# A selective-attention and SwiGLU kernel on one Trainium2 core: a reordered first batch, bias rows issued by GpSimd, delayed stores

## The chip, the cores and the metric

The kernel runs on one core of one Trainium2 chip. The core has five engines with a queue each, which run in parallel and meet at semaphores: TensorE (PE; its weight loads are listed apart as PEld), VectorE (DVE), ScalarE (ACT), GpSimd (POOL) and SyncE (SP), which here only issues DMAs. 16 DMA engines move data between device memory and the on-chip memory SBUF. Matrix products land in PSUM, eight banks per partition, and are read from there by DVE and ACT. The metric is device microseconds of one execution. Each engine works through its own queue in program order; an instruction that waits holds up all behind it on that engine.

## What is computed

Eight batches of eight heads of causal attention over 576 positions with head size 64; a bias made of a cumulative sum of the positive part of `s` is added to the scores. The result, as 4608 tokens of width 512, goes through a SwiGLU block with 1536 hidden features.

```python
scores = scale * np.matmul(q, k.transpose(0, 1, 3, 2))
cum = np.cumsum(np.maximum(s, 0.0), axis=-1)
bias = -(cum[:, :, :, None] - cum[:, :, None, :])
scores = np.where(causal, -1000000000.0, scores + np.minimum(bias, 0.0))
attn = np.exp(scores - np.max(scores, axis=-1, keepdims=True))
attn = attn / (np.sum(attn, axis=-1, keepdims=True) + 1e-09)
x = heads side by side of np.matmul(attn, v)
g = x @ w_gate
out = (g * (1.0 / (1.0 + np.exp(-g))) * (x @ w_val)) @ w_out
```

## The kernel before

**Layout.** The 64 heads are handled in 16 blocks of four (`hb`, or `h` in the later loops). The two tile pairs `KQ[hb % 2][r]` hold the transposed k and q of a block: for r = 0 and 1 two heads, in 64 of 128 partitions. Four of the other 64 partitions hold bias rows: high and low part of the cumulative sum and constants, so that the score matmul (L347) adds the bias by itself. The rest of them has to be zero; memsets at the start see to it (L203 and L209 on GpSimd, L204 on ACT, which multiplies the tile of ones `one_s` by 0). `aug` (L180 to L188) sends the four bias rows of a block from `HL` to `KQ` with four DMAs. `HL` comes from `s` through a chain on VectorE (L213 to L217), whose cumulative sum takes `one_s` too.

**Preparing a block.** `load_qk` loads k and q in float32, `cast_one` or `cast_half` turn them to bfloat16 (tiles `ck`, `cq`). For blocks 0 to 4 TensorE transposes them (`pe_transpose`, L272; `pe_transpose_half`, L286) and `pe_out` copies from PSUM to `KQ`, on DVE (L301) or ACT (L299). `prep_one` is one such transpose with its DVE and its ACT copy. For blocks 5 to 15, `scratch` writes the cast tiles to device memory (L244), `transposes` reads them back with transposing DMAs (L254), and `split` copies them to `KQ` on DVE (L259). `load_v` loads V of a batch in five pieces (L164), into one buffer; `cast_v` casts them to `VT` (L171). `init_vt` sets the ones column and the zero border of `VT`.

**A head.** `score_piece` makes the scores of a head in four pieces, the exps on ACT (L360) and the causal masks on GpSimd (L363 for four diagonal blocks, L368 for the last small one). In the first batch two pieces share a two-bank PSUM tile and one exp. `av_piece` multiplies by V (L385), `av_out` divides by the row sums (L401, L402), and `x_pe` transposes a pair of heads (L420) and copies the result to the FFN's input `xt` (L424, L425).

**Order.** The program writes the order out by hand: the order of the calls is the order in each queue. `first_batch` (L588 to L620) runs heads 0 to 7 alone. In it a dictionary `avq` says after which head's scores which products come, and `wq` when GpSimd loads the FFN weights (L315, float32 to bfloat16). After that, for each of nine FFN tiles of 512 tokens, `ffn_items` yields 36 times, and between its pieces `pump` runs pieces of `attn_items` for the next batch: in proportion to the count n of yields, from n0 on (7 in the first tile). `hook` hangs preparation on certain n of the first tile. `side` places loads, casts, bias rows, scratch writes and DMA transposes by the head's number in its block (`step`). An FFN tile has 12 feature blocks of gate (L518, tanh on ACT at L523, first product on DVE at L525) and value (L533, second product `ht` on DVE at L538), then four output blocks (L546), each scaled on ACT (L554) and stored by SyncE (L556).

Of the kernel before, what the change touches and what calls it, by code (L numbers as in the profile page):

```python
# [19 lines left out]
def kernel(  # L20
# [11 lines left out]
    nc = tc.nc  # L32
# [60 lines left out]
    VT = [const.tile([128, NCH, H, D + 1], BF16, name=f"vt{i}") for i in range(2)]  # L93
    ident = const.tile([128, 128], BF16)
    s_sb = const.tile([BH, S], FP32)
    one_s = const.tile([BH, S], FP32)
    c8 = const.tile([BH, S], FP32)
    HL = const.tile([BH, 4, 2, S], BF16)
    warm = const.tile([128, 1], FP32)
# [1 line left out]
    with tc.manual_schedule():  # L101
# [52 lines left out]
        def load_qk(hb):  # L154
            load_one(hb, "k")
            load_one(hb, "q")
# [31 lines left out]
                )  # L188

        nc.sync.dma_start(s_sb, s.rearrange("b h n -> (b h) n"))  # L190
        for r in range(NR):
            load_one(0, "k", (r, r + 1))
            load_one(0, "q", (r, r + 1))
        load_qk(1)

        nc.vector.memset(warm, 0.0)
        nc.scalar.activation(warm, warm, AF.Exp)
        nc.vector.memset(one_s, 1.0)
        nc.vector.memset(HL[:, 0:2, 0, :].bitcast(FP32), ONES2)
        nc.vector.memset(HL[:, 2:4, 1, :].bitcast(FP32), NEGS2)  # L200
        make_identity(nc, ident)
        for r in range(2):
            nc.gpsimd.memset(aug_rows(0, r), 0.0)  # L203
            nc.scalar.mul(  # L204
                KQ[1][r][64 * (1 - r) : 64 * (1 - r) + 64, 0, :],
                one_s[:, 0:1].to_broadcast([64, NR * S + 64]), 0.0,
            )
        for r in range(2):
            nc.gpsimd.memset(aug_rows(1, r)[:, 1, :], 0.0)  # L209
            for i in range(2):  # L210
                nc.gpsimd.memset(KQ[i][r][64 * r : 64 * r + 64, :, NR * S :], 0.0)

        nc.vector.tensor_scalar(s_sb, s_sb, 0.0, 8.0, ALU.max, ALU.mult)  # L213
        nc.vector.tensor_tensor_scan(c8, one_s, s_sb, 0.0, ALU.mult, ALU.add)
        nc.vector.tensor_copy(HL[:, 0, 1, :], c8)
        nc.vector.tensor_sub(HL[:, 1, 1, :], c8, HL[:, 0, 1, :])
        nc.vector.tensor_copy(HL[:, 2:4, 0, :], HL[:, 0:2, 1, :])  # L217

        SP4 = [nc.sync] * 4

        cts = {}

# [170 lines left out]
        def av_out(bh):  # L393
# [13 lines left out]
            give(bs)  # L407
            pts.pop(bh)

        def x_pe(pr):  # L410
            b, r = divmod(pr, H // 2)
            ot = ots.pop(pr)
            for tt in ((0, 1) if b == 0 else (b + 1,)):
                if r == 0:
                    xts[tt] = xtp.tile([128, 4, TT], BF16, tag="xt", name="xt")
# [12 lines left out]
        def side(h, step):  # L428
            bh = HB * h + step
            if bh == 8:  # L430
                w_load("o", 0)
            if bh == 10:
                w_load("o", 1)
            if bh == H:
                for c in range(5):
                    cast_v(1, c, nc.gpsimd)
            if h >= 3 and h + 3 < NHB and step == 0:
                load_qk(h + 3)
            if h + 1 < NHB and h + 1 >= NPE:
                if step == 0:  # L440
                    split(h + 1, "k", nc.vector)
                    aug(h + 1, SP4)
                if step == 1:
                    split(h + 1, "q", nc.vector)
            if h + 2 < NHB and h + 2 >= NPE:
                if step == 1:
                    cast_one(h + 2, "k", nc.gpsimd)
                if step == 2:
                    cast_one(h + 2, "q", nc.gpsimd)
                    scratch(h + 2)  # L450
                if step == 3:
                    transposes(h + 2)
            bn = h // 2 + 1
            if 2 <= bn < B:
                if h % 2 == 0:
                    if step == 2:
                        load_v(bn, (0, 1))
                    if step == 3:
                        load_v(bn, (2, 3, 4))
                else:  # L460
                    if step == 1:
                        cast_v(bn, 0, nc.gpsimd)
                        cast_v(bn, 1, nc.gpsimd)
# [10 lines left out]
            pe_out(hb, nm, g, 0, nc.vector)  # L474
            pe_out(hb, nm, g, 1, nc.scalar)

        PREP_AT = {(0, 3): 0, (1, 3): 1, (2, 1): 2, (2, 3): 3}

        def attn_items():
            for kk in range(H, BH + 2):  # L480
                h, step = divmod(kk, HB)
                if kk < BH:
# [1 line left out]
                        cast_one(h + 2, "k", nc.gpsimd)  # L484
                        cast_one(h + 2, "q", nc.gpsimd)
                    if step == 0 and 3 < h + 1 < NPE:
                        aug(h + 1, SP4)
                    for ci in range(4):
                        score_piece(kk, ci)
                        if ci == 1:  # L490
                            side(h, step)
                        yield kk + 0.1 + ci / 8
                        if h + 1 < NPE and (step, ci) in PREP_AT:
                            prep_one(h + 1, PREP_AT[step, ci])
                            yield kk + 0.1 + ci / 8
                x = kk - 2
                if x >= H and x % 2 == 1:
                    x_pe(x // 2)
                    yield kk + 0.5
                p = kk - 1  # L500
                if H <= p < BH:
# [5 lines left out]
                    av_out(p)  # L507
                    yield kk + 0.8

        def ffn_items(tt):  # L510
            xt = xts[tt]
            hts = []
            for ft in range(NFT):
                j, f0 = divmod(ft * 128, WCH)
                gbs = take()
# [26 lines left out]
            for ts_ in range(4):  # L542
                ybs = take()
                py = view(ybs, DM)
                for ft in range(NFT):
# [7 lines left out]
                ysb = yp.tile([128, DM], FP32, tag="y", name="ysb")  # L553
                nc.scalar.mul(ysb, py, 0.5)  # L554
                give(ybs)
                nc.sync.dma_start(  # L556
                    out[tt * TT + ts_ * 128 : tt * TT + (ts_ + 1) * 128, :], ysb
                )
                yield 1

        def init_vt(i):
            nc.gpsimd.memset(VT[i][:, :, :, D : D + 1], 1.0)
            nc.gpsimd.memset(VT[i][64:128, 4, :, 0:D], 0.0)

        cast_half(0, "k", 0, nc.scalar)
        cast_half(0, "q", 0, nc.gpsimd)
        aug(0, SP4)
        load_v(0, range(5))
        load_qk(2)
        aug(1, [nc.gpsimd] * 4)  # L570
        for nm in ("k", "q"):
            for g in range(2):
                pe_transpose_half(0, nm, g, 0)
        pe_out(0, "k", 0, 0, nc.scalar)
        pe_out(0, "k", 1, 0, nc.scalar)
        pe_out(0, "q", 0, 0, nc.vector)
        pe_out(0, "q", 1, 0, nc.scalar)
        cast_half(0, "k", 1, nc.scalar)
        cast_half(0, "q", 1, nc.vector)
        for nm, eng in (("k", nc.scalar), ("q", nc.vector)):  # L580
            for g in range(2):
                pe_transpose_half(0, nm, g, 1)
                pe_out(0, nm, g, 1, eng)
        cast_one(1, "k", nc.gpsimd)
        cast_one(1, "q", nc.vector)
        init_vt(0)

# [39 lines left out]
        def pump(upto):  # L627
# [3 lines left out]
                except StopIteration:  # L631
                    state["pos"] = 1e9

        LAG = 1.65
        hook = {
            1: [lambda: cast_one(2, "k", nc.gpsimd), lambda: cast_one(2, "q", nc.vector)],
            2: [lambda: prep_one(2, 0)],
            3: [lambda: prep_one(2, 1)],
            4: [lambda: prep_one(2, 2)],
            5: [lambda: prep_one(2, 3)],  # L640
            8: [lambda: cast_one(3, "k", nc.gpsimd), lambda: cast_one(3, "q", nc.gpsimd)],
            21: [lambda: load_qk(5)],
        }
        for tt in range(NTT):
            lo = H * (tt + 1) + (LAG if tt else 0)
            hi = min(H * (tt + 2) + LAG, BH + 2)
# [39 lines left out]
```

The softmax here doesn't subtract the row's maximum and nothing guards it: scores larger than these inputs give would overflow.

## Time and profile before

| | us |
|---|---|
| median of 13 runs (lowest, highest) | 409.43 (406.83, 410.7) |
| the profiled execution, whole | 410.7 |
| its span in the profile | 409.0 |
| first score matmul | 11.26 |
| last piece of V 0 landed | 25.30 |
| first FFN matmul | 37.73 |
| last matmul ends | 405.29 |
| PE busy from 100 to 300 | 198.3 of 200 |

The span is the stretch from the first to the last instruction that the profile shows. Busy time is shown by engine; a busy TensorE at a granted clock of 0.50 does half the work. "Landed" is when an instruction that waits for a DMA can go on. In groups of instructions a line reads: line, engine, operation, what is written and read, count, busy time, mean, and the idle time before with what ended it.

### The profile page before, as it was taken

How to read it: one execution, taken by the hardware profiler on the slowest of the kernel's cores; microseconds unless marked ns; L12 is line 12 of the kernel's file. 1: busy time of each engine (PE TensorE's matmuls, PEld its weight loads, DVE VectorE, ACT ScalarE, POOL GpSimd, SP SyncE). 2: the span in 40 equal slices, each digit the busy share in tenths (PEclk: the TensorE clock that was granted, in tenths of full speed). 3: DMA queues.
4: the chain of work that ended last, by engine and by line, in shares of the span. 5: the costliest groups of instructions: out<-in, count | busy, mean ns of one | idle time of the engine just before them, and what ended most of it. 6: DMA issues, size and time to landing. Idle time of an engine off the chain costs nothing.

```text
span 409.0 us, 7999 instructions
## 1 busy us (share of the span) xinstructions
PE 381.2 (93%) x3047; PEld 213.2 (52%) x3100; DVE 249.1 (61%) x487; ACT 212.1 (52%) x407; POOL 125.5 (31%) x225
## 2 busy tenths in 40 slices
PE   3747798999999999999999999999999999999996
PEld 2545355665555555555555555555555554444442
DVE  7726666746873688358844884579447743752860
ACT  7823567766554555456545564565555542322321
POOL 6943263643252226131623162316211110000000
PEclk9959989999999999999999999999999999999999
DMA  7999899487745693469346926690520002002002
GB/s 245 161 257 213 272 158 217 185 253 194 193 116 182 165 229 101 129 220 231 101 122 210 262 78 109 217 183 30 116 80 0 2 27 78 0 7 98 2 1 103
DMA packets 85288, 56.71 MB, mean 139 GB/s; under 512 B 65489, under 2 KB 69553, under 8 KB 85249
## 3 DMA queue, kind: packets, MB, share of 16 engines
q1 hardware_dynamic: 81440, 51.44, 45.9%
q0 software_dynamic: 3808, 4.76, 7.0%
q8 instruction: 24, 0.39, 0.4%
q14 instruction: 16, 0.12, 0.1%
HBM read 37.90 MB, written 15.93 MB: 132 GB/s over the span
## 4 chain that ended last, share of the span: by engine, by line
PE 85%; DVE 5%; DMA 3%; ACT 2%; issue 2%; SPq 1%; POOL 0%; ACTq 0%; DVEq 0%
PE bank L546 23%; PE bank L518 21%; PE bank L533 21%; PE bank L347 9%; PE bank L385 7%; DMA rawv<-in_v_dram 3%; PE bank L420 3%; ACT th L523 1%; DVE kq L301 1%; DVE pp L525 1%; PE one L385 1%; DVE ht L538 1%; DMA s_sb<-in_s_dram 1%; ACT kq L299 1%; PE wide L347 1%
## 5 line engine op out<-in xcount | busy, mean ns | idle before, releaser
L360 ACT ACTIVATE pt<-bank 128x512 bf16<-128x512 f32 x224 | 104.2, 505 | 42.4 <-PE bank L347 35.1
L525 DVE SCALAR_TENSOR_TENSOR pp<-th,bank 128x512 bf16<-128x512 bf16 x108 | 74.2, 687 | 64.3 <-ACT th L523 63.8
L518 PE MATMUL bank<-xt,wg 128*128 128x512 bf16 x417 | 110.4, 380 | 1.5 <-DVE xt L425 0.7
L533 PE MATMUL bank<-xt,wv 128*128 128x512 bf16 x410 | 109.9, 381 | 1.1
L523 ACT ACTIVATE th<-bank 128x512 bf16<-128x512 f32 x108 | 64.6, 598 | 80.7 <-PE bank L518 78.9
L546 PE MATMUL bank<-wo,ht 128*128 128x512 bf16 x416 | 103.5, 379 | 0.9
L363 POOL TENSOR_SCALAR_AFFINE_SELECT pt<-pt 128x512 bf16<-128x512 bf16 x64 | 40.8, 638 | 126.4 <-ACT pt L360 126.3
L538 DVE TENSOR_TENSOR ht<-pp,bank 128x512 bf16<-128x512 bf16 x108 | 73.8, 684 | 7.4
L347 PE MATMUL bank<-kq 128*128 128x128 bf16 (+4 forms) x504 | 66.7, 241 | 3.6 <-DVE kq L301 2.9
L347 PEld LDWEIGHTS <-kq 128*128 128x128 bf16 x576 | 46.1, 100 | 43.9 <-issue 8.0
L518 PEld LDWEIGHTS <-wg 128*128 128x128 bf16 x432 | 38.5, 98 | 36.5 <-issue 1.3
L533 PEld LDWEIGHTS <-wv 128*128 128x128 bf16 x432 | 38.8, 98 | 34.5 <-issue 0.6
L546 PEld LDWEIGHTS <-ht 128*128 128x128 bf16 x432 | 38.2, 98 | 34.9
L385 PEld LDWEIGHTS <-pt 128*128 128x128 bf16 x960 | 41.6, 99 | 19.0 <-issue 1.9
L385 PE MATMUL bank<-vt,pt 128*128 128x65 bf16 x840 | 44.0, 194 | 0.0
L554 ACT ACTIVATE ysb<-bank 128x512 f32<-128x512 f32 x36 | 21.5, 598 | 42.9 <-PE bank L546 41.4
L368 POOL TENSOR_SCALAR_AFFINE_SELECT pt<-pt 128x64 bf16<-128x64 bf16 x64 | 15.3, 239 | 63.4 <-ACT pt L360 60.7
L402 DVE TENSOR_TENSOR ot<-bank,rc 128x320 bf16<-128x320 f32 x56 | 27.5, 491 | 1.9
L424 DVE COPY xt<-bank 128x128 bf16<-128x128 bf16 (+6 forms) x28 | 9.0, 321 | 31.7 <-PE bank L420 31.0
L171 POOL CAST vt<-rawv 128x512 bf16<-128x512 f32 (+1 forms) x40 | 25.9, 673 | 3.6 <-DMA rawv<-in_v_dram 3.6
L401 DVE RECIPROCAL rc<-bank 128x5 f32<-128x5 f32 x56 | 10.6, 190 | 25.2 <-PE bank L385 25.2
L230 POOL CAST ck<-rawk 128x1152 bf16<-128x1152 f32 x15 | 17.4, 1159 | 10.6 <-DMA rawk<-in_k_dram 10.6
(59 smaller groups left out, 192.5 us busy)
## 6 DMA issues: line engine op xcount, KB each, us to landing
out_dram<-ysb SPq DMA_DIRECT2D x36, 256.0 KB
rawk<-in_k_dram SPq DMA_DIRECT2D x15, 576.0 KB
rawq<-in_q_dram SPq DMA_DIRECT2D x15, 576.0 KB
rawv<-in_v_dram SPq DMA_DIRECT2D x32, 256.0 KB
ks<-ck SPq DMA_DIRECT2D x11, 288.0 KB
qs<-cq SPq DMA_DIRECT2D x11, 288.0 KB
wg<-in_moe_w_gate_dram POOLq DMA_DIRECT2D x2, 768.0 KB, 12.4
wv<-in_moe_w_val_dram POOLq DMA_DIRECT2D x2, 768.0 KB, 12.7
```

The lines of the kernel that those rows point to most:

```text
L171: eng.tensor_copy(VT[b % 2][0:n, c, :, 0:D], loaded["v", b][0:n, c, :, :])
L347: nc.tensor.matmul(sc[:, o : o + w], T[:, 1, e * S + 128 * tj : e * S + 128 * (tj + 1)], T[:, 0, e * S + lo : e * S + hi], start=True, sto ...
L360: nc.scalar.activation(pt[:, c0 : c0 + W], sc[:, 0:W], AF.Exp, scale=0.125)
L363: nc.gpsimd.affine_select(pt[:, 1088:1600], pt[:, 1088:1600], pattern=[[0, 4], [1, 128]], compare_op=ALU.is_ge, fill=zreg, base=0, channel ...
L385: nc.tensor.matmul(av[:, bi * (D + 1) : (bi + 1) * (D + 1)], pt[:, c0 : c0 + 128], VT[b % 2][:, tj, h, :], start=(tj == 0), stop=(tj == bi),)
L402: nc.vector.tensor_mul(ot[:, :, e * D : (e + 1) * D], av3[:, :, 0:D], rc[:, :, None].to_broadcast([128, NCH, D]),)
L518: nc.tensor.matmul(pg, WG[j][:, c, f0 : f0 + 128], xt[:, c, :], start=(c == 0), stop=(c == 3),)
L523: nc.scalar.activation(th, pg, AF.Tanh, scale=0.5)
L525: nc.vector.scalar_tensor_tensor(pp, in0=th, scalar=1.0, in1=pg, op0=ALU.add, op1=ALU.mult)
L533: nc.tensor.matmul(pv, WV[j][:, c, f0 : f0 + 128], xt[:, c, :], start=(c == 0), stop=(c == 3),)
L538: nc.vector.tensor_mul(ht, pp, pv)
L546: nc.tensor.matmul(py, hts[ft][:, ts_ * 128 : (ts_ + 1) * 128], WO[ft // WKO][:, ft % WKO, :], start=(ft == 0), stop=(ft == NFT - 1),)
```

## The change

It touches four places.

*The start.* `one_s` becomes one column, read by broadcast. The memsets are dealt out anew: ACT clears half of the rows of `KQ[0]` instead of `KQ[1]`, GpSimd the other half; `KQ[1]` is cleared by VectorE (r = 0) and GpSimd (r = 1); both `init_vt` move to the start. The load of q 1 moves behind the bias rows of block 0. Some casts and copies of blocks 0 and 1 change engine.

*The first batch.* The products come later: product 0 after the scores of head 5, products 1 and 2 after head 6, product 3 after head 7, and 4 to 7 after a loop that now holds scores in the main. Block 1 is transposed one head later. The last two pieces of V 0 are cast by DVE. k 3 and q 3 are loaded ahead of V 1, and both right after block 2's bias rows. The second Wg load comes after head 4 instead of 3, Wo is loaded at the end of the batch. Block 2 is cast in the batch, and two of its four transposes run there, with their copies on ACT.

*The first FFN tile.* It has the two remaining transposes of block 2, at n = 1 and 2; `n0` is 4. (`LAGS` has the values that the former expression gave, `PREP_AT` gives what it gave for h = 2 and 3, and the new bound in `H <= x < BH` cuts nothing off.)

*Later.* Bias rows of blocks 1 and 4 to 15 are issued by GpSimd (block 1's were before). The DMA transposes of a block move from step 3 to step 0 of the next block, the scratch writes from step 2 to step 3, the DVE copies from steps 0 and 1 to steps 2 and 3. A store is issued when the next result has been written, the last tile's at once.

```diff
@@ start
-    one_s = const.tile([BH, S], FP32)
+    one_s = const.tile([128, 1], FP32)
...
+        def init_vt(i):
+            nc.gpsimd.memset(VT[i][:, :, :, D : D + 1], 1.0)
+            nc.gpsimd.memset(VT[i][64:128, 4, :, 0:D], 0.0)
+
...
-        load_qk(1)
+        load_one(1, "k")
...
+        def pads(i):
+            for r in range(2):
+                nc.gpsimd.memset(KQ[i][r][64 * r : 64 * r + 64, :, NR * S :], 0.0)
+
         for r in range(2):
-            nc.gpsimd.memset(aug_rows(0, r), 0.0)
+            nc.gpsimd.memset(aug_rows(0, r)[:, 1, :], 0.0)
             nc.scalar.mul(
-                KQ[1][r][64 * (1 - r) : 64 * (1 - r) + 64, 0, :],
-                one_s[:, 0:1].to_broadcast([64, NR * S + 64]), 0.0,
+                KQ[0][r][64 * (1 - r) : 64 * (1 - r) + 64, 0, :],
+                one_s[0:64, 0:1].to_broadcast([64, NR * S + 64]), 0.0,
             )
-        for r in range(2):
-            nc.gpsimd.memset(aug_rows(1, r)[:, 1, :], 0.0)
-            for i in range(2):
-                nc.gpsimd.memset(KQ[i][r][64 * r : 64 * r + 64, :, NR * S :], 0.0)
+        pads(0)
+        init_vt(0)
+        init_vt(1)
+        nc.vector.memset(aug_rows(1, 0), 0.0)
+        nc.gpsimd.memset(aug_rows(1, 1), 0.0)
+        pads(1)
...
+        GP4 = [nc.gpsimd] * 4
@@ side
-            if bh == 8:
-                w_load("o", 0)
-            if bh == 10:
-                w_load("o", 1)
...
                 if step == 0:
+                    transposes(h + 1)
+                    aug(h + 1, GP4)
+                if step == 2:
                     split(h + 1, "k", nc.vector)
-                    aug(h + 1, SP4)
-                if step == 1:
+                if step == 3:
                     split(h + 1, "q", nc.vector)
...
                 if step == 2:
                     cast_one(h + 2, "q", nc.gpsimd)
+                if step == 3:
                     scratch(h + 2)
-                if step == 3:
-                    transposes(h + 2)
@@ ffn_items
+            for f in stores:
+                f()
+            stores.clear()
...
-                nc.sync.dma_start(
-                    out[tt * TT + ts_ * 128 : tt * TT + (ts_ + 1) * 128, :], ysb
-                )
+                for f in stores:
+                    f()
+                stores.clear()
+                stores.append(
+                    lambda a=tt * TT + ts_ * 128, y=ysb: nc.sync.dma_start(
+                        out[a : a + 128, :], y
+                    )
+                )
+                if tt == NTT - 1:
+                    stores.pop()()
@@ before the first batch
-        cast_half(0, "q", 0, nc.gpsimd)
+        cast_half(0, "q", 0, nc.scalar)
         aug(0, SP4)
+        load_one(1, "q")
         load_v(0, range(5))
         load_qk(2)
-        aug(1, [nc.gpsimd] * 4)
...
-        pe_out(0, "q", 1, 0, nc.scalar)
+        pe_out(0, "q", 1, 0, nc.vector)
         cast_half(0, "k", 1, nc.scalar)
-        cast_half(0, "q", 1, nc.vector)
+        cast_half(0, "q", 1, nc.gpsimd)
+        aug(1, GP4)
...
-        cast_one(1, "k", nc.gpsimd)
+        cast_one(1, "k", nc.vector)
         cast_one(1, "q", nc.vector)
-        init_vt(0)
@@ first_batch
-            avq = {4: (0,), 5: (1, 2), 6: (3, 4), 7: (5, 6, 7)}
-            wq = {0: ("g", 0), 1: ("v", 0), 3: ("g", 1), 5: ("v", 1)}
+            avq = {5: (0,), 6: (1, 2), 7: (3,)}
+            wq = {0: ("g", 0), 1: ("v", 0), 4: ("g", 1), 5: ("v", 1)}
...
-                if h == 1:
+                if h == 2:
                     order = [(nm, g) for g in range(2) for nm in ("k", "q")]
...
-                if h == 2:
+                    for c in range(3, 5):
+                        cast_v(0, c, nc.vector)
+                if h == 3:
                     for c in range(3):
                         cast_v(0, c, nc.gpsimd)
-                if h == 3:
-                    for c in range(3, 5):
-                        cast_v(0, c, nc.gpsimd)
                     aug(2, SP4)
+                    load_qk(3)
+                    load_v(1, range(5))
+                if h == 6:
+                    cast_one(2, "k", nc.gpsimd)
+                if h == 7:
+                    aug(3, SP4)
+                    load_qk(4)
                 for p in avq.get(h, ()):
                     av_piece(p, range(NCH))
                     av_out(p)
-                    if p % 2 == 0 and p:
-                        x_pe(p // 2 - 1)
-            init_vt(1)
-            aug(3, SP4)
-            load_v(1, range(5))
-            load_qk(3)
-            load_qk(4)
-            x_pe(H // 2 - 1)
+            cast_one(2, "q", nc.gpsimd)
+            w_load("o", 0)
+            w_load("o", 1)
+            x_pe(0)
+            for p in (4, 5, 6, 7):
+                av_piece(p, range(NCH))
+                av_out(p)
+                if p == 5:
+                    x_pe(1)
+                if p == 6:
+                    x_pe(2)
+                if p >= 6:
+                    nm = ("k", "q")[p - 6]
+                    pe_transpose(2, nm, 0)
+                    for r in range(2):
+                        pe_out(2, nm, 0, r, nc.scalar)
+            x_pe(3)
@@ first FFN tile
-            1: [lambda: cast_one(2, "k", nc.gpsimd), lambda: cast_one(2, "q", nc.vector)],
-            2: [lambda: prep_one(2, 0)],
-            3: [lambda: prep_one(2, 1)],
-            4: [lambda: prep_one(2, 2)],
-            5: [lambda: prep_one(2, 3)],
-            8: [lambda: cast_one(3, "k", nc.gpsimd), lambda: cast_one(3, "q", nc.gpsimd)],
+            1: [lambda: prep_one(2, 2)],
+            2: [lambda: prep_one(2, 3)],
+            3: [lambda: cast_one(3, "k", nc.gpsimd), lambda: cast_one(3, "q", nc.gpsimd)],
             21: [lambda: load_qk(5)],
...
-            n0 = 7 if tt == 0 else 0
+            n0 = 4 if tt == 0 else 0
```

More of the change, by code (lines that the diff above doesn't have):

```diff
@@ L193 @@
             load_one(0, "q", (r, r + 1))
-        load_qk(1)
+        load_one(1, "k")
         nc.vector.memset(warm, 0.0)
+        nc.vector.memset(one_s, 1.0)
         nc.scalar.activation(warm, warm, AF.Exp)
-        nc.vector.memset(one_s, 1.0)
         nc.vector.memset(HL[:, 0:2, 0, :].bitcast(FP32), ONES2)
@@ L201 @@
         make_identity(nc, ident)
+        def pads(i):
+            for r in range(2):
+                nc.gpsimd.memset(KQ[i][r][64 * r : 64 * r + 64, :, NR * S :], 0.0)
         for r in range(2):
-            nc.gpsimd.memset(aug_rows(0, r), 0.0)
+            nc.gpsimd.memset(aug_rows(0, r)[:, 1, :], 0.0)
             nc.scalar.mul(
-                KQ[1][r][64 * (1 - r) : 64 * (1 - r) + 64, 0, :],
-                one_s[:, 0:1].to_broadcast([64, NR * S + 64]), 0.0,
-            )
-        for r in range(2):
-            nc.gpsimd.memset(aug_rows(1, r)[:, 1, :], 0.0)
-            for i in range(2):
-                nc.gpsimd.memset(KQ[i][r][64 * r : 64 * r + 64, :, NR * S :], 0.0)
+                KQ[0][r][64 * (1 - r) : 64 * (1 - r) + 64, 0, :],
+                one_s[0:64, 0:1].to_broadcast([64, NR * S + 64]), 0.0,
+            )
+        pads(0)
[4 more added lines that the diff above has]
+        pads(1)
         nc.vector.tensor_scalar(s_sb, s_sb, 0.0, 8.0, ALU.max, ALU.mult)
-        nc.vector.tensor_tensor_scan(c8, one_s, s_sb, 0.0, ALU.mult, ALU.add)
+        nc.vector.tensor_tensor_scan(
+            c8, one_s[0:BH, 0:1].to_broadcast([BH, S]), s_sb, 0.0, ALU.mult, ALU.add
+        )
         nc.vector.tensor_copy(HL[:, 0, 1, :], c8)
@@ L408, in av_out, with x_tiles @@
             pts.pop(bh)
+        def x_tiles(b, r):
+            for tt in ((0, 1) if b == 0 else (b + 1,)):
+                if r == 0:
+                    xts[tt] = xtp.tile([128, 4, TT], BF16, tag="xt", name="xt")
         def x_pe(pr):
@@ L412, in x_pe @@
             ot = ots.pop(pr)
-            for tt in ((0, 1) if b == 0 else (b + 1,)):
-                if r == 0:
-                    xts[tt] = xtp.tile([128, 4, TT], BF16, tag="xt", name="xt")
+            x_tiles(b, r)
             bs = take()
@@ L475, in prep_one @@
             pe_out(hb, nm, g, 1, nc.scalar)
-        PREP_AT = {(0, 3): 0, (1, 3): 1, (2, 1): 2, (2, 3): 3}
+        PREP_AT = {
+            2: {(0, 3): 0, (1, 3): 1, (2, 1): 2, (2, 3): 3},
+            3: {(0, 3): 0, (1, 3): 1, (2, 1): 2, (2, 3): 3},
+        }
         def attn_items():
@@ L486, in attn_items @@
                     if step == 0 and 3 < h + 1 < NPE:
-                        aug(h + 1, SP4)
+                        aug(h + 1, GP4)
                     for ci in range(4):
@@ L492, in attn_items @@
                         yield kk + 0.1 + ci / 8
-                        if h + 1 < NPE and (step, ci) in PREP_AT:
-                            prep_one(h + 1, PREP_AT[step, ci])
+                        if (step, ci) in PREP_AT.get(h, ()):
+                            prep_one(h + 1, PREP_AT[h][step, ci])
                             yield kk + 0.1 + ci / 8
                 x = kk - 2
-                if x >= H and x % 2 == 1:
+                if H <= x < BH and x % 2 == 1:
                     x_pe(x // 2)
@@ L508, in attn_items @@
                     yield kk + 0.8
+        stores = []
         def ffn_items(tt):
@@ L555, in ffn_items @@
                 give(ybs)
-                nc.sync.dma_start(
-                    out[tt * TT + ts_ * 128 : tt * TT + (ts_ + 1) * 128, :], ysb
-                )
+                for f in stores:
[5 more added lines that the diff above has]
+                    )
+                )
+                if tt == NTT - 1:
+                    stores.pop()()
                 yield 1
-        def init_vt(i):
-            nc.gpsimd.memset(VT[i][:, :, :, D : D + 1], 1.0)
-            nc.gpsimd.memset(VT[i][64:128, 4, :, 0:D], 0.0)
         cast_half(0, "k", 0, nc.scalar)
-        cast_half(0, "q", 0, nc.gpsimd)
+        cast_half(0, "q", 0, nc.scalar)
         aug(0, SP4)
+        load_one(1, "q")
         load_v(0, range(5))
         load_qk(2)
-        aug(1, [nc.gpsimd] * 4)
         for nm in ("k", "q"):
@@ L632, in pump @@
                     state["pos"] = 1e9
-        LAG = 1.65
+        LAGS = [0] + [1.65] * NTT
         hook = {
-            1: [lambda: cast_one(2, "k", nc.gpsimd), lambda: cast_one(2, "q", nc.vector)],
-            2: [lambda: prep_one(2, 0)],
-            3: [lambda: prep_one(2, 1)],
-            4: [lambda: prep_one(2, 2)],
-            5: [lambda: prep_one(2, 3)],
-            8: [lambda: cast_one(3, "k", nc.gpsimd), lambda: cast_one(3, "q", nc.gpsimd)],
+            1: [lambda: prep_one(2, 2)],
+            2: [lambda: prep_one(2, 3)],
+            3: [lambda: cast_one(3, "k", nc.gpsimd), lambda: cast_one(3, "q", nc.gpsimd)],
             21: [lambda: load_qk(5)],
@@ L644 @@
         for tt in range(NTT):
-            lo = H * (tt + 1) + (LAG if tt else 0)
-            hi = min(H * (tt + 2) + LAG, BH + 2)
+            lo = H * (tt + 1) + LAGS[tt]
+            hi = min(H * (tt + 2) + LAGS[tt + 1], BH + 2)
             span = 36
-            n0 = 7 if tt == 0 else 0
+            n0 = 4 if tt == 0 else 0
             n = 0
```

## The prediction

> **What bounds the kernel now.** I read the engine row and the tensor engine's row of 40 slices first, then the clock row.
>
> ```profile
> PE 381.2 (93%) x3047; PEld 213.2 (52%) x3100; DVE 249.1 (61%) x487; ACT 212.1 (52%) x407; POOL 125.5 (31%) x225
> ...
> PE   3747798999999999999999999999999999999996
> ...
> PEclk9959989999999999999999999999999999999999
> ```
>
> TensorE is busy 381.2 of 409.0 us. Its idle time, and all of its time at half clock, lies in the first seven slices (some 70 us). A table of stretches says the same: 99.16 us busy of 100 between 200 and 300. So a change can win only in the front, or lose anywhere. The front in stretches of 2 us (columns: stretch and length, then busy time and instructions of PE, PEld, DVE, ACT, POOL, then granted clock, DMA share, GB/s):
>
> ```profile
> 20.00:22.00 2.00, 0.26 (x7) 0.15 (x5) 0.38 (x1) 0.83 (x2) 1.80 (x4) 0.50 1.17 205
> 22.00:24.00 2.00, 0.29 (x5) 0.18 (x4) 0.00 (x0) 0.00 (x0) 0.00 (x0) 0.50 1.13 227
> 24.00:26.00 2.00, 0.00 (x0) 0.00 (x0) 0.00 (x0) 0.00 (x0) 0.65 (x2) 0.50 1.11 279
> 26.00:28.00 2.00, 1.98 (x22) 1.64 (x22) 0.69 (x2) 0.88 (x1) 0.75 (x2) 0.50 1.10 277
> ...
> 46.00:48.00 2.00, 0.11 (x1) 0.00 (x0) 0.59 (x2) 1.32 (x2) 1.15 (x1) 1.00 1.03 395
> 48.00:50.00 2.00, 0.93 (x9) 0.74 (x11) 1.53 (x3) 0.98 (x2) 1.15 (x1) 1.00 0.74 281
> 50.00:52.00 2.00, 2.00 (x14) 1.33 (x14) 1.38 (x2) 2.00 (x5) 1.10 (x2) 0.53 0.02 7
> ```
>
> Two holes are to be seen, at 20 to 26 and at 46 to 49, each with half clock after it. The chain of waits, and then the list of who waited for whom (total us, times, longest), name their causes:
>
> ```profile
> 14.30 11.00 DMA rawv<-in_v_dram
> 25.30 0.05 issue
> 25.35 0.62 POOL vt L171
> 26.02 0.21 PE one L385
> 26.23 1.33 PE wide L347 x9
> ```
>
> ```profile
> ACT kq L299 <- DVE kq L301: 14.3, 11, 2.7
> ...
> PE one L385 <- POOL vt L171: 5.5, 2, 3.7
> ...
> POOL vt L171 <- DMA rawv<-in_v_dram: 3.6, 1, 3.6
> ...
> PE bank L347 <- DVE kq L301: 2.9, 1, 2.9
> ```
>
> The first hole: the attention-value product of head 0 (L385) stands in PE's order ahead of the scores of head 5, and waits for the last piece of V 0, which lands at 25.3. The second: the scores of head 8 wait for the transposes of block 2, whose copies from PSUM pass by turns through DVE (L301) and ACT (L299) between the work of the first FFN tile.
>
> **Up to V 0.** q 1 is issued behind the first bias rows, directly ahead of V 0, not at 3.97 us. In the SyncE timeline the bias rows are issued from 8.31 to 11.2 and V's five pieces from 11.23. DMA moved 45 GB/s at 10 to 12 and was back at 277 at 13.0, so those bytes were free before and now stand in front of V: 0.59 MB (576 KB) / 0.28 MB/us (277 to 283 GB/s at 26 to 30) = 2.1 us. V then lands at about 27.4. No row shows V behind q 1 with both weight loads beside it. Low bound: unchanged, 25.3, if the weight transfers and not the order set the landing. High bound: the first load of Wv takes at most 15.0 us from its issue at 16.39, to 31.4; if the last 0.7 of V's 1.18 MB wait until then, they take 2.5 us more, to 33.9. I take 27.4, since bytes have to be moved in any order, and the second Wg load, issued a head later now, doesn't come between. The cast of V's last piece moves from GpSimd to VectorE behind block 1's eight copies (5.64 us, to about 22), so it is idle when V lands: 0.61 us as before. Product 0 ends at 28.1 (26.2 before).
>
> Ahead of that all else has cover. The scores of head 5 and their exps (1.6 us) move into the wait. The q cast of the first half goes to ACT (5.97 to 6.63, where GpSimd's stood at 5.97 too) and holds the first k copy back by 0.45 us. The second half goes from DVE at 8.88 to an idle GpSimd. Casts of block 1 go to DVE, the q one not before about 15, and block 1's copies end about 1.5 us later, at 22. Memsets: GpSimd's early list is 2 x 0.60 + 4 x 0.28 + 2 x 0.81 for V's borders + 1.13, done at about 6.5; DVE's 1.14 us for block 1 replace 0.54 for the ones and end at 3.4, ahead of the 3.85 at which the chain from s can start. With the cover of the V wait (5 us, from 22 to 27) gone, these would cost at most the 1.5 us.
>
> **From V 0 to the FFN.** Before, 26.2 to 37.73 held scores and exps of heads 5 to 7, eight products and four output transposes: 11.5 us. After, PE does the scores of head 6 (1.5 at half clock, L347 at 26.05), products 1 and 2 (1.84 at half clock), scores 7 (0.87), product 3 (0.53): 32.9. Then VectorE sets the pace: per head a reciprocal and a multiplication (0.71), per pair two copies (0.51). In order: head 3, pair 0, heads 4, 5, pair 1, head 6, pair 2, head 7 are 5 x 0.71 + 3 x 0.51 = 5.1; with the last transposes (0.53), their copies (0.51) and four handovers (0.5 together) 39.5. PE has 6 x 0.53 and the two moved block-2 transposes (0.88) beside it and fits; ACT's four copies for them (4 x 0.73) end near 40.4, before the first tanh can start (39.5 + 1.1). So FFN 0 starts at 39.5 for 37.73: **+1.8**.
>
> **In FFN tile 0.** The two transposes done early take **-0.88** of PE time from it. Of four ping-pong copies two are left: PE reaches head 8's scores after 5 half-steps of 0.86 and 2 x 0.44 = 5.2 us; the copies run tanh, product, DVE copy, ht, DVE copy, ACT copy: 1.1 + 0.6 + 0.69 + 0.75 + 0.68 + 0.75 + 0.73 = 5.3 us. The wait of 2.9 us thus goes to 0.1: **-2.8**. With it goes the half clock of 50.1 to 53.6, in which PE was busy all of 3.5 us for 1.75 us of work: **-1.75**. [...] PE idled another 1.3 us between 58 and 66 around block 3's copies; these stay, and I count 0 (bounds -1.3 and 0).
>
> **The rest.** Bias rows on GpSimd: from the page's rows 4 x 0.63 = 2.5 us once in four heads, on an engine busy 31%. Behind them in its queue stands the small mask (L368), for which the product waits. In the steady part a small mask ended at 150.05 and the product's last part ran at 155.90: 5.9 us of slack over 2.5. Cost 0; without that slack 12 blocks x 2.5 = 30 us at most. [...]
> SyncE loses these issues (2.9 us in four heads) and sends each store a step later, when the result is ready; its 137.6 us of waiting for results delayed only loads that PE never waited for. Results have three buffers and a store is sent one step (some 5 us) later: 0. The DMA transposes move one head later, their copies two, still one head ahead of the scores (5 us for copies of 0.5 to 1 us): 0. k 3 and q 3 no longer queue behind the bias rows of block 3 (until 33.96): GpSimd's wait of 9.3 us for k 3 had no PE behind it, 0. Wo's loads go out before FFN 0, some 20 us ahead of use at 8 to 15 us each: 0. The last stores go out at once, so the tail is the same.
>
> **Sum:** 1.8 - 0.88 - 2.8 - 1.75 = **-3.6 us**. The profiled execution, 409.0 of span within 410.7, goes to 405.4 of span. It is the slowest of the 13; from their median of 409.43 the sum gives **405.8 us**.
>
> **Rivals.** Less than 0.3% (1.2 us) can't be told from no change.
> (a) The forecast, 404 to 408: chance 0.52.
> (b) V is not late: the weight loads set its landing, which the 205 to 279 GB/s beside it speak for. The FFN starts 2.1 us earlier: 403.7. Against it: DMA was full from 13 on. 0.20.
> (c) The hole at 46 stays: the first tile is bound by ACT and DVE, not by the number of copies; the 14.3 us that ACT waited for DVE copies speak for it. Then 1.8 - 0.88 = +0.9: 410.3. Against it: half of the copies are gone. 0.10.
> (d) Slower: V 0 starves beside the weight loads. Its last piece, 128 KB, came 4 us or more after the one before while both ran. Each us of landing beyond 27.4 costs one; from 31.0 the gain is gone, and at 33.9 it is 405.8 + 6.5 = 412.3. Against it: c0 to c2 hold GpSimd's third weight load back, so the competitors run dry. 0.18.
>
> The likeliest is (a). The range takes in (b) with the 1.3 us of the later idle time, to 402, and (c) and the nearer part of (d), to 411. Faster is (a) and (b), 0.72; the same is (c), 0.10; slower is (d), 0.18.
>
> **What would show it.** V's last cast at 27 to 28, on DVE; no product before it; exps of six heads ahead of it; the first FFN matmul at 39 to 40; no PE hole over 0.5 us in the 10 us after and full clock there; PE over 99% from 70 us on. V at 25 or beyond 31 makes it (b) or (d); POOL named in the waits of L385 after 70 us would make the bias rows wrong.

## The result, and the profile after

| | before | after |
|---|---|---|
| median, us (runs) | 408.75 (48) | 413.76 (11) |
| ratio, 95% interval | 1 | 1.013 (1.0107 to 1.0153) |
| span of the profiled execution | 409.0 | 412.3 |
| last piece of V 0 landed | 25.3 | 29.9 |
| first FFN matmul | 37.73 | 41.37 |
| last piece of V 1 cast | 55.2 | 58.1 |
| PE busy from 100 to 300 | 198.3 | 198.3 |

The change makes the kernel 1.3% slower; 405.8 us and a gain had been forecast. The medians are 5.0 us apart and the two profiled spans 3.3: the profiled execution of the kernel before (410.7 us) lies 2 us above its median, that of the changed kernel (414.04) 0.3 us. The traces below account for the 3.3; what makes executions of one kernel differ by the rest they don't show. The page of the changed kernel first, engine row, then PE in 40 slices and the clock:

```profile
PE 381.7 (93%) x3046; PEld 213.9 (52%) x3100; DVE 244.9 (59%) x488; ACT 213.3 (52%) x409; POOL 153.5 (37%) x270
...
PE   4728969999999999999999999999999999999996
...
PEclk9978989999999999999999999999999999999999
```

PE's busy time is the same to 0.5 us, and past slice 7 nothing differs: the whole loss lies in the front again. The front in stretches of 2 us (PE, PEld, DVE, ACT, POOL busy; clock; DMA share; GB/s):

```profile
22.00:24.00 2.00, 0.29 (x8) 0.20 (x6) 0.26 (x1) 1.40 (x2) 0.00 (x0) 1.00 1.15 198
24.00:26.00 2.00, 0.00 (x0) 0.00 (x0) 0.00 (x0) 0.00 (x0) 0.00 (x0) 1.00 1.19 235
26.00:28.00 2.00, 0.00 (x0) 0.00 (x0) 0.00 (x0) 0.00 (x0) 0.61 (x2) 0.64 1.21 220
28.00:30.00 2.00, 0.59 (x9) 0.47 (x9) 0.86 (x2) 0.00 (x0) 1.99 (x5) 0.50 1.05 331
...
46.00:48.00 2.00, 2.00 (x20) 1.26 (x19) 0.87 (x2) 1.98 (x5) 0.00 (x0) 1.00 1.21 198
...
52.00:54.00 2.00, 0.72 (x11) 0.59 (x10) 1.34 (x3) 2.00 (x6) 0.00 (x0) 1.00 1.24 249
54.00:56.00 2.00, 0.25 (x3) 0.16 (x3) 1.36 (x3) 0.71 (x2) 0.90 (x2) 1.00 0.98 196
56.00:58.00 2.00, 1.51 (x11) 0.83 (x10) 0.48 (x1) 0.14 (x1) 1.44 (x3) 0.82 0.13 23
58.00:60.00 2.00, 1.68 (x10) 1.03 (x11) 0.90 (x3) 0.60 (x1) 1.19 (x5) 0.50 0.64 151
```

The hole of 46 to 49 is gone, as forecast, and its half clock with it. The hole ahead of V 0 is longer, and a new one lies at 52 to 58, with half clock behind it. In the stretches shown up to 54 the DMA share is 1.05 to 1.24; between 56 and 60 it is 0.13 and 0.64. The wait lists of the changed kernel name both (its L361, L399 and L540 are L347, L385 and L518 of before):

```profile
POOL vt L171 <- DMA rawv<-in_v_dram: 13.0, 5, 6.6
...
DVE vt L171 <- DMA rawv<-in_v_dram: 6.9, 2, 6.7
...
PE one L399 <- POOL vt L171: 5.8, 1, 5.8
...
PE bank L399 <- POOL vt L171: 3.4, 2, 2.6
...
PE bank L540 <- ACT kq L313: 1.4, 1, 1.4
```

"one" is the product in the first batch, which waits for V 0; "bank" is head 8's product, which waits for V 1: a second landing that had hidden before. The fifth line is a small new wait at the start of the FFN. The SyncE timeline shows how the landings became late (start, length, what, count):

```profile
11.40 12.18 SPq L164 DMA_DIRECT2D rawv<-in_v_dram  x5
23.62 1.28 SPq L147 DMA_DIRECT2D rawk<-in_k_dram  x1
24.94 1.85 SPq L147 DMA_DIRECT2D rawq<-in_q_dram  x1
26.90 2.85 SPq L185 DMA_DIRECT2D kq<-HL  x4
29.84 0.39 SPq L147 DMA_DIRECT2D rawk<-in_k_dram  x1
30.33 0.41 SPq L147 DMA_DIRECT2D rawq<-in_q_dram  x1
31.17 23.16 SPq L164 DMA_DIRECT2D rawv<-in_v_dram  x5
```

Issuing V 0's five pieces takes 12.18 us, where it took 4.47; the chain of waits puts 7.68 of them on the fifth piece alone, which waits for no result; the loads of k 3 and q 3, issued at 29.84 and 30.33, took 0.39 and 0.41 us. What held the fifth piece the profile doesn't show; that it was the transfers in front of it is the author's reading. With q 1 moved (e1 below) the five took 4.35 us, with the weights moved (e2) 5.68. All behind it in the queue (k 2, q 2, bias rows, k 3, q 3, V 1) is late too: V 1's five issues take 23.16 us.

### The profile page after: what moved, and what is told of

It is laid out like the page before. It is cut to its first block, busy times and chain, and to the rows that moved or that the text cites. A ratio compares the mean times of both kernels' runs of the same rounds, so it can differ in the third digit from the quotient of the medians.

```text
span 412.3 us, 7994 instructions
## 1 busy us (share of the span) xinstructions
PE 381.7 (93%) x3046; PEld 213.9 (52%) x3100; DVE 244.9 (59%) x488; ACT 213.3 (52%) x409; POOL 153.5 (37%) x270
## 4 chain that ended last, share of the span: by engine, by line
PE 83%; SPq 7%; DMA 5%; DVE 2%; issue 1%; ACT 1%; POOL 0%; ACTq 0%; DVEq 0%
PE bank L568 22%; PE bank L540 21%; PE bank L555 21%; PE bank L361 9%; PE bank L399 7%; SPq L164 6%; DMA rawv<-in_v_dram 3%; PE bank L437 2%; DMA rawq<-in_q_dram 2%; DMA s_sb<-in_s_dram 1%; SPq L185 1%; SPq L147 0%; DVE pp L547 0%; DVE c L225 0%; DVE kq L315 0%
## 5 line engine op out<-in xcount | busy, mean ns | idle before, releaser
L540 PE MATMUL bank<-xt,wg 128*128 128x512 bf16 x417 | 110.9, 381 | 2.4 <-ACT kq L313 1.4
L361 PEld LDWEIGHTS <-kq 128*128 128x128 bf16 x576 | 47.3, 101 | 40.0 <-issue 5.0
L361 PE MATMUL bank<-kq 128*128 128x128 bf16 (+4 forms) x504 | 66.3, 241 | 0.7 <-ACT kq L313 0.4
L540 PEld LDWEIGHTS <-wg 128*128 128x128 bf16 x432 | 38.5, 98 | 37.2 <-issue 2.3
L399 PEld LDWEIGHTS <-pt 128*128 128x128 bf16 x960 | 41.5, 99 | 27.4 <-issue 10.3
L399 PE MATMUL bank<-vt,pt 128*128 128x65 bf16 x840 | 44.3, 194 | 3.8 <-POOL vt L171 3.4
L382 POOL TENSOR_SCALAR_AFFINE_SELECT pt<-pt 128x64 bf16<-128x64 bf16 x64 | 18.2, 284 | 37.8 <-ACT pt L374 37.2
L185 POOL DMA_DIRECT2D kq<-HL x52 | 30.6, 589 | 1.6 <-issue 0.4
L171 POOL CAST vt<-rawv 128x512 bf16<-128x512 f32 (+1 forms) x38 | 24.6, 670 | 13.0 <-DMA rawv<-in_v_dram 13.0
```

Of the source, the lines that this page charges most:

```text
L185: engs[hh].dma_start(KQ[hb % 2][r][r0 : r0 + 4, :, e * S : (e + 1) * S], HL[bh : bh + 1, :, :, :],)
L361: nc.tensor.matmul(sc[:, o : o + w], T[:, 1, e * S + 128 * tj : e * S + 128 * (tj + 1)], T[:, 0, e * S + lo : e * S + hi], start=True, sto ...
L399: nc.tensor.matmul(av[:, bi * (D + 1) : (bi + 1) * (D + 1)], pt[:, c0 : c0 + 128], VT[b % 2][:, tj, h, :], start=(tj == 0), stop=(tj == bi),)
L540: nc.tensor.matmul(pg, WG[j][:, c, f0 : f0 + 128], xt[:, c, :], start=(c == 0), stop=(c == 3),)
```

## The experiments

Each kernel is the changed one with the edit shown, unless said otherwise. Ratios are to the kernel before, on the same chip, with their 95% interval.

| label | median us | ratio (interval) | first FFN matmul | PE hole after 42 |
|---|---|---|---|---|
| after | 413.76 | 1.013 (1.011 to 1.015) | 41.37 | 52 to 58 |
| e1_q1_front | 412.22 | 1.008 (1.006 to 1.011) | 36.42 | 48 to 54 |
| e2_weights_late | 414.40 | 1.014 (1.011 to 1.017) | 33.90 | 48 to 57 |
| e3_wo_late | 411.00 | 1.005 (1.003 to 1.007) | 40.70 | none |
| e4_v1_first | 419.83 | 1.028 (1.025 to 1.031) | 42.46 | 49 to 58 |
| e5_q1_wo | 406.74 | 0.996 (0.994 to 0.999) | 38.64 | none |
| e6_all_dma | 409.08 | 1.002 (0.999 to 1.004) | 35.63 | 48 to 52 |
| e7_late_undone | 413.84 | 1.013 (1.009 to 1.016) | 41.87 | 53 to 57 |
| e8_before_weights_late | 408.99 | 1.001 (0.998 to 1.003) | 33.77 | 42 to 48 |
| e9_due_order | 407.19 | 0.998 (0.995 to 1.000) | 32.73 | 44 to 47 |
| e10_due_order_n7 | 407.16 | 0.995 (0.993 to 0.998) | 35.19 | 48 to 50 |
| e11_due_order_w_early | 406.17 | 0.995 (0.992 to 0.998) | 36.84 | none |
| e12_products_early | 406.72 | 0.999 (0.995 to 1.002) | 36.02 | 46 to 49, part |

"None" is no stretch of 2 us after 42 with less than 1.3 us of PE.

**q 1 in front again (e1).**

```diff
-        load_one(1, "k")
+        load_qk(1)
...
-        load_one(1, "q")
         load_v(0, range(5))
```

> The changed kernel with q 1 loaded right behind k 1 again, ahead of the bias rows of block 0. Theory A (the 0.59 MB of q 1 stand in front of V 0): the last piece of V 0 lands 2 us or more earlier than its 29.8, the first FFN matmul moves from 41.4 to 39.5 or less, and the time falls from 413.8 to 411 or 412. Theory B (the weight loads, not q 1, hold V 0 back): V 0 still lands at 29 or later and the time stays within 1 us of 413.8.

V 0's issues took 4.35 us and its last piece was cast at 25.18; the FFN began at 36.42, 5 us earlier. Theory A has its landing. The time fell by 1.5 us only, since the next hole took the rest. In the stretches of this kernel:

```profile
48.00:50.00 2.00, 0.11 (x2) 0.02 (x1) 1.90 (x4) 1.17 (x4) 0.00 (x0) 1.00 1.22 206
50.00:52.00 2.00, 0.00 (x0) 0.00 (x0) 0.42 (x1) 0.75 (x1) 0.00 (x0) 1.00 1.17 248
52.00:54.00 2.00, 0.33 (x3) 0.21 (x3) 0.00 (x0) 0.00 (x0) 0.89 (x2) 0.56 0.46 99
```

V 1's last two pieces were cast from 55.05 on, for 56.90 in the changed kernel: a landing that moves by 1.9 us, met 5 us earlier.

**Weights late (e2), and the same on the kernel before (e8).**

```diff
-            wq = {0: ("g", 0), 1: ("v", 0), 4: ("g", 1), 5: ("v", 1)}
+            wq = {3: ("g", 0), 4: ("v", 0), 5: ("g", 1), 6: ("v", 1)}
```

> The changed kernel with the four loads of Wg and Wv behind the scores of heads 3, 4, 5 and 6 in place of 0, 1, 4 and 5; q 1 stays where the change put it. Theory B (weight loads beside V 0 hold it back): V 0 lands at 19 to 22, its five issues take less than 5 us, the first FFN matmul comes at 35 to 37, and the time falls by 4 us or more, if the weights are there in time. Theory A (q 1 in front): V 0 gains 1 us at most and the time stays above 412.

> The kernel before with Wg and Wv behind heads 3, 4, 5 and 6 and nothing else changed. If the weight loads hold V 0 back there too: V 0 lands at 17 to 19 instead of 25.3, no hole at 20 to 26, and 3 to 5 us less than before, some 404. If V 0's landing was set by its own small packets: within 1 us of before.

With q 1 still in the way, V 0 is no longer waited for at all. SyncE and DVE of e2:

```profile
11.38 5.68 SPq L164 DMA_DIRECT2D rawv<-in_v_dram  x5
...
24.33 25.75 SPq L164 DMA_DIRECT2D rawv<-in_v_dram  x5
```

```profile
22.39 1.74 DVE L171 CAST vt<-rawv 128x512 bf16<-128x512 f32 x2
```

So theory B has the landing too: V 0 was late since q 1 *and* the weights stood beside it, and either edit is enough. Of e2's other expectations the issues missed (5.68 us for less than 5) and the FFN came earlier than said (33.90 for 35 to 37). Both kernels reach the FFN 4 to 7.5 us earlier, and by their medians neither is faster. In e2 V 1's pieces took 25.75 us to issue. In e8, which does not have the change at all, PE idled some 4 us between 42 and 48. Most of that is the hole of the kernel before at 46 to 49, met 4 us earlier:

```profile
45.03 0.83 PE L347 MATMUL bank<-kq 128*128 128x128 bf16 x8 [2.89 <-DVE kq L301]
```

Only some 1.2 us more, ahead of 47.92, belong to k 3, for which GpSimd waited 13.6 us. No half clock followed this hole:

```profile
44.00:46.00 2.00, 0.91 (x9) 0.72 (x11) 1.55 (x3) 0.96 (x2) 0.00 (x0) 1.00 1.03 354
46.00:48.00 2.00, 0.84 (x6) 0.30 (x6) 1.38 (x2) 2.00 (x5) 1.15 (x1) 1.00 1.04 396
```

The expectations of 4 us less failed in both medians. The profiled execution of e8, its fastest, has a span 4.0 us shorter than that of the kernel before, so where e8's median keeps the 4 us the traces don't show.

**Wo late (e3), and both landings mended (e5: the edits of e1 and e3).**

```diff
-            w_load("o", 0)
-            w_load("o", 1)
             x_pe(0)
...
+            if bh == 8:
+                w_load("o", 0)
+            if bh == 10:
+                w_load("o", 1)
```

> The changed kernel with the two loads of Wo at heads 8 and 10 again. Theory C (Wo's 3.1 MB of reads beside V 1 make V 1 late): V 0 as in the changed kernel, V 1's last cast at 50 or earlier instead of 57, the PE hole between 52 and 58 gone, and 4 to 5 us less: 409 to 410. Theory D (V 1 is late since k 3 and q 3 and a held-up SyncE queue stand in front of it): 1 us less at most.

> The changed kernel with q 1 in front again and Wo at heads 8 and 10 again, both other edits of the DMA order kept. If two late landings (V 0 behind q 1 and Wg/Wv, V 1 beside Wo) are the whole loss: V 0 at about 25, first FFN matmul at 36 to 37, V 1 ahead of its use, no PE hole over 1.5 us after 45, and 404 to 406, faster than before by about 1%. If something else in the change costs too (bias rows on GpSimd, the ping-pong copies, the late stores): 408 or more with a hole that names it.

V 1 in e3, issued by SyncE and cast by GpSimd without a wait:

```profile
30.38 14.54 SPq L164 DMA_DIRECT2D rawv<-in_v_dram  x5
```

```profile
48.80 2.83 POOL L171 CAST vt<-rawv 128x512 bf16<-128x512 f32 x5
```

The hole is gone and V 1 is in time: theory C. V 1's last cast ended at 51.6 for the 50 expected, as GpSimd came to it only at 48.80. The gain is 2.8 us by the medians for an expected 4 to 5 (4.9 between the two profiled spans, 412.3 and 407.4), with V 0 as late as ever. By the medians the two edits are worth 1.5 and 2.8 us alone and 7.0 us together. That one alone lets the other landing take part of it back is to be seen in e1's longer second hole; that the two together are worth more than their sum is not clear of the intervals. In e5 the FFN began at 38.64 for the 36 to 37 expected. Together the edits undo the loss, and the rest of the change then stands at 0.996 (0.994 to 0.999). 406.74 lies just outside the 404 to 406 expected.

**V 1 ahead of k 3 and q 3 (e4).**

```diff
-                    load_qk(3)
                     load_v(1, range(5))
+                    load_qk(3)
```

> The changed kernel with V 1 loaded ahead of k 3 and q 3. Theory D: V 1 lands some 4 us earlier (1.18 MB at about 0.28 MB/us), the hole between 52 and 58 shrinks to 2 us or less, and the time falls by 3 to 4 us to about 410. Theory C: V 1 still stands beside Wv's second half and Wo; the hole stays above 4 us and the time above 412.

Neither theory had this. V 1's issues ended at 43.5 for 54.3, but its last piece landed at 54.8 for 57.3 in the changed kernel, and for 48.2 in e3: beside the weights it was late at both places in the queue, as theory C has it, and theory D is not the main cause. The time got worse for another reason. V 1 was no longer waited for, but GpSimd's queue held the cast of k 3 (at n = 3) ahead of head 8's mask and V 1's casts:

```profile
56.32 1.15 POOL L244 CAST ck<-rawk 128x1152 bf16<-128x1152 f32 x1 [16.48 <-DMA rawk<-in_k_dram]
...
59.57 2.83 POOL L171 CAST vt<-rawv 128x512 bf16<-128x512 f32 x5
```

The wait of 16.5 us is for k 3; V 1's casts behind it ran without one of their own. The order of the loads and that of the instructions that wait for them have to move together.

**Everything in the order of need (e6, e9, e10, e11, e12).** e6 has the edits of e1, e2 and e3. e9 adds V 1 ahead of k 3 and q 3, with their casts after V 1's:

```diff
             if bh == H:
                 for c in range(5):
                     cast_v(1, c, nc.gpsimd)
+                cast_one(3, "k", nc.gpsimd)
+                cast_one(3, "q", nc.gpsimd)
...
-            2: {(0, 3): 0, (1, 3): 1, (2, 1): 2, (2, 3): 3},
+            2: {(1, 1): 0, (1, 3): 1, (2, 1): 2, (2, 3): 3},
...
-            3: [lambda: cast_one(3, "k", nc.gpsimd), lambda: cast_one(3, "q", nc.gpsimd)],
```

and Wo at heads 9 and 11, block 2's casts at heads 5 and 6, its two early transposes behind products 4 and 5. e10 is e9 with `n0 = 7`, e11 is e9 with the weights at heads 0, 1, 4, 5, and e12 is e11 with the products where they were before the change (and the two early transposes behind products 5 and 6).

> The same with Wg and Wv behind heads 3, 4, 5 and 6 as well. If V 0 is then out of the way (landed by 20), no PE hole between 22 and 30, first FFN matmul at 33 to 34. If the DMA engines as a whole are the bound of the front, the bytes that were moved back come due later: V 1 or the second halves of Wg and Wv are late, with a hole between 40 and 55 again, and the time is no better than that of the kernel with q 1 in front and Wo late. If not: 402 to 403.

> The kernel with q 1 in front, all weights late (Wg and Wv behind heads 3 to 6, Wo at heads 9 and 11), V 1 ahead of k 3 and q 3, whose casts and first transpose come after V 1's casts, and block 2's casts and two early transposes a little earlier. Theory (the front is a queue of bytes, and only their order by when they are needed is free): V 1 lands before 46, the hole at 48 to 52 is gone, the first FFN matmul no longer waits 1.4 us for ACT's copies, and the time is 403 to 405, faster than before by 1%. If the bytes are bound whatever their order: a new late landing (second halves of Wg and Wv, k 3) with a hole of 3 us or more, and 407 to 409.

> The same with attention of batch 1 starting at n = 7 of the first FFN tile, as before the change, in place of 4. If V 1's landing still decides: less hole at 46 to 52 and 1 us or more faster than with 4. If V 1 is in time anyway: within 1 us.

> The kernel with q 1 in front and V 1 ahead of k 3 and q 3 as above, but Wg and Wv at heads 0, 1, 4 and 5 as the change has them. If weights beside V 0 cost their hole there and win it back later: V 0 at 25, first FFN matmul at 36 to 37 and no hole later, 404 to 406; slower than with late weights by 1 us or more if the order by need is right.

> The kernel with weights early, q 1 in front and V 1 ahead of k 3 and q 3, with the attention-value products back at their places before the change (product 0 ahead of the scores of head 5, 5 to 7 and their output transposes inside the loop). If scores ahead of products are worth what the prediction counted on (one head's scores and exps, 1.6 us or more, inside the wait for V 0): first FFN matmul 1 to 2 us later than 36.8 and 407.5 to 408.5. If the order of the products is worth nothing: within 1 us of 406.2.

e6 reached the FFN 3 us before e5 and was not faster: V 1's last piece was late again (GpSimd waited 4.6 us for it). In e9 V 1 came in time, and the hole was k 3, a new late landing as the expectation's second branch has it, with 407.19 in its 407 to 409:

```profile
46.58 0.45 PE L286 MATMUL bank<-ident,ck 128*128 128x128 bf16 x5 [2.67 <-POOL ck L244]
```

By ratio e10 and e11 are the fastest, 0.5% under the kernel before with intervals that exclude 1, as e5's does; the 403 to 405 hoped for was not reached. Against e9 their intervals overlap. e11, with the weights early again, was no slower than e9, so that the order of need is best for every load is not shown. e12 against e11 is inconclusive: the FFN began 0.8 us earlier, not later, and the medians differ by 0.55 us with overlapping intervals. So no gain is shown for the later products, the main edit of the first batch.

**The steady part undone (e7).**

```diff
-                    transposes(h + 1)
-                    aug(h + 1, GP4)
-                if step == 2:
                     split(h + 1, "k", nc.vector)
+                    aug(h + 1, SP4)
...
-                if tt == NTT - 1:
-                    stores.pop()()
+                stores.pop()()
```

and the scratch writes, transposes and copies at their former steps.

> The changed kernel with its steady part undone: bias rows of blocks 4 to 15 by SyncE, DMA transposes, scratch writes and copies at their former steps, stores at once. By the prediction these cost nothing either way: within 1.5 us of 413.8. If GpSimd's bias rows hold the masks back and so TensorE: 3 us or more less.

413.84 for 413.76, PE busy 99.16 of 100 between 100 and 200 in both: taken together, bias rows, transposes and stores neither cost nor bring more than the interval of these four runs (about 1.4 us either way). One by one they were not tried.

## Why the prediction was wrong, point by point

- **The bound.** Right that only the front could win or lose. Missed: that from 13 us to past 50 the front has two bounds, TensorE's order and a queue of bytes (DMA share 1.05 to 1.26 in each 2 us from 14 to 54 of the changed kernel). The DMA share above 1, read in the very stretches quoted (1.10 to 1.17 from 20 to 28), was a sign that a byte moved forward may push another back, as V 0's landing moved from 25.3 to 29.9.
- **"Wo's loads go out before FFN 0, some 20 us ahead of use at 8 to 15 us each: 0."** This is the step that failed. It asked when Wo is needed, and not what stands beside it: V 1 does. In the changed kernel head 8's product waited 2.6 + 0.8 us for V 1's casts and 0.4 us for a mask behind them, and 56 to 62 ran at 0.82, 0.50 and 0.83 of the clock, which on 1.51, 1.68 and 1.95 us of busy time loses an estimated 1.4 us, if work goes as the clock (four gate matmuls took 1.91 us from 58.88, at 0.50 for most of it, and 1.03 us from 62.19, at 1.00): 5.3 us in all. e3, which moves nothing but Wo, shows V 1 in time and no hole. How the weights hold V 1 back can be read from the DMA queues of the changed kernel between 44 and 52 (packets, MB, busy share):

```profile
q0 software_dynamic: 1235, 1.25, 91.5%
q1 hardware_dynamic: 1236, 0.31, 29.7%
```

q0 has GpSimd's weight loads, about 1010 bytes a packet (1.25 MB in 1235) on the bfloat16 side, q1 V 1's rows, about 250 bytes a packet (0.31 MB in 1236). The two moved as many packets, and V 1 got a fifth of the bytes of this count, 0.31 MB in 8 us. With no weights beside it, between 13.0 and 14.5 of the kernel before, V moved 0.41 MB in 1.5 us.
- **V 0, +2.1 us.** The mechanism was right (e1) and the size wrong: 29.9 for 27.4 (high bound 33.9). GpSimd's memsets and the earlier first scores also moved the first weight load from 14.80 to 13.25, and V 0 had no stretch to itself. The forecast had each effect and priced q 1 by its bytes alone, at 0.28 MB/us. e1 and e2 show that the lateness takes both.
- **First FFN matmul.** 39.5 forecast, 41.37 measured: 2.5 from V 0's landing and a new wait, less about 1.5 because the chain from product 0 to the last output copy ran faster than reckoned. The new wait: the first gate matmul stood until ACT's four copies were done (41.32). The prediction let them end before the first *tanh*; but the FFN's banks belong to a second PSUM pool, which replaces the first, and its first matmul waited for the last readers of the first pool (1.36 us for ACT's copies). Against the copy of the FFN's input that ended at 40.56 this costs 0.8 us. In e9 to e12, with these transposes earlier or otherwise placed, the wait is for that copy alone.
- **The hole at 46 and the half clock after it: -2.8 and -1.75.** Both right: PE was busy 2.00 of 2 us in each stretch from 42 to 48, at a clock of 1.00 up to 56. The -1.75 had some luck in it. In the kernel before the clock fell after 2.91 us without a matmul and about 1 us of work, and with the hole gone it did not fall; but in e8 the same hole of 2.89 us was followed by a clock of 1.00, so the half clock belongs to this trace's hole and not to every hole of its length, and what the clock goes by is not shown.
- **The sum.** From the first FFN matmul to the end the forecast was -5.4 us; it came to 370.9 for 371.3, -0.3. The 5.3 us of the V 1 hole make up this difference of 5.1 but for 0.2. With +3.6 for the FFN's start the -0.3 gives the +3.3 between the two spans: 412.3, where 405.4 had been forecast.
- **The rest at 0.** e7 agrees for bias rows, transposes and stores together, to about 1.4 us. GpSimd issued 52 bias rows at 589 ns each on average, none above 702.
- **The rivals.** (d) had the right kind, a landing starved by weights, and named V 0 and Wg/Wv; its own price at 29.9 would have been 408.3. The landing that decided, V 1, was in no rival.

What stays open: no kernel here took bytes away, so that the queue of bytes is *the* bound of the front rests on the holes that moved in e1, e2, e6 and e9.

## What to carry to other kernels

Where the DMA share stands at 1 or more, as it did here (1.05 to 1.26 from 14 to 54), no load that is moved earlier should be taken as free, however long before its use it is (e11 shows that some are nearly so): list all loads of the stretch by the time at which something waits for them, and price each move by the landing that it pushes back, the next hidden one included. A hole that closes shows the next landing: two late landings may each be worth little alone (1.5 and 2.8 us here), and only mending both undid the loss (7.0; that this is more than the sum is not clear of noise). And a load moved in its queue wants the instructions that wait for it moved in theirs (e4 moved the load alone: 419.83 for 413.76).

## What the hardware showed that was not expected

- One DMA issue of a piece of V kept SyncE 7.68 us, and five issues kept it 12.18 and 23.16 us (4.47 and 6.99 before), without a wait for a result that the profile shows (1.6 us in all for SyncE from 10 to 60): the time lies in the *issue*, and what stood behind it in the queue went out later (k 2 at 23.62 for 15.75 before).
- Beside the float32-to-bfloat16 weight loads V 1's rows moved as many packets as these (1236 and 1235 from 44 to 52 of the changed kernel), at about 250 bytes for 1010, and got 0.31 MB against 1.25. The profile counts a weight load by its bfloat16 side (768 KB for a half of Wg, which is 1536 KB in float32), so the 194 to 198 there do not compare with the 254 to 286 of V 0 alone (13.0 to 14.5 before) or the 378 to 413 of k and q alone (46 to 49 before).
- A clock of 0.50 came in or right after an idle stretch of 2.91 us (before), of 2.67 us (e9) and of 5.76 us (after), but not with one of 2.89 us (e8). In e9 it also came between 32 and 36, where no idle stretch of the 4 us before was longer than 1.01 us.
